# Transposes placed elsewhere in the first two chunks of a fused linear-attention and MLP kernel

## The chip, the cores and the metric

The kernel runs on one core of one Trainium2 chip. The metric is the device time of one execution in microseconds (us); the kernel before took 219.26 us, the median of 3 runs (218.94 to 219.39). Five engines work side by side, each through its own list of instructions in order: PE (matrix products and transposes), ACT (ScalarE: functions and copies), DVE (VectorE: elementwise work), POOL (GpSimd: elementwise work, and the issuing of loads) and SP (SyncE, which issues the first loads, the stores and some transposing transfers). They wait for each other by semaphores. PE writes only to PSUM, a small memory of eight banks, from which ACT and DVE read.

## The reference, cut to what matters

A linear attention with decay in blocks, and then a two-layer MLP with a periodic activation:

```python
batch, n_heads, seq, head_dim = (4, 8, 768, 64)      # q, k, v
n_tokens, d_model, d_ff = (3072, 512, 2048)          # the MLP
...
        intra = np.einsum('bhic,bhjc->bhij', qb, kb) * Dmask[None]
        intra = np.einsum('bhij,bhjd->bhid', intra, vb)
        inter = np.einsum('bhid,bhde->bhie', qb * lam_pow[None], kv_state)
        out[:, :, sl] = intra + inter
        ...
        kv_state = lam_block[None, :, None, None] * kv_state + np.einsum('bhsd,bhse->bhde', kb_dec, vb)
...
    h = x @ w_in
    s = np.sin(alpha * h)
    g = h + s * s / (alpha + 1e-09)
    return (g @ w_out).astype(np.float32)
```

## The kernel before

The sequence of 768 tokens is cut into six chunks of 128 tokens. One chunk of one of the four batches is called a unit, `u = 4 * chunk + batch`: units 0 to 3 are the first chunk, 4 to 7 the second. The program writes out the order of each engine by hand.

**A unit's attention.** `transposes(u)` (line 173) turns k and q of all eight heads by eight PE transposes, first four of k and then four of q, into one PSUM tile `QK_ps`, which ACT copies to `QKT` (line 183). `scores(u)` (line 196) makes eight products k times q into `F_ps` (PSUM tag `pf`), and DVE multiplies them with the decay mask to `STm` (line 209). `intra_mm(u)` (line 244) multiplies v with `STm` into `O_ps` (tag `po`), `inter_mm(u)` (line 254) adds q times the running state `kv`, and DVE's `copy_x(u)` (line 261) scales the sum into the unit's columns of `xt`, the input of the MLP. In the first chunk there is no state yet, and `first_out(u)` (line 345) does the products and the copy together.

**A chunk's MLP.** For a chunk `g` the 2048 hidden features are 16 slices ("sixteenths") of 128. `hidden(g, f)` (line 278) makes four products over the four batches' 512 tokens into a bank `hps`; ACT takes the sine (line 286) and, mostly, the square (line 289), and `finish(g, f)` (line 292) adds on DVE into `gall`. The banks for `hps` rotate, from the tenth sixteenth on over three tags h0, h1, h2 (line 275), so `hidden(f)` waits for `finish(f - 3)`. `project(g, n)` (line 305) multiplies `gall` with `w_out`; `hidden` of a chunk needs all of its `xt`.

**The start.** Until the first chunk's `xt` is complete there is no MLP work. k and q of unit 0 come through SP and are cast by DVE (lines 334 and 341); k, q and v of the others are loaded by POOL's queue, one after the other. Unit 0's k and q are transposed into a bank each and copied each for itself (lines 363 to 369); units 1 to 3 use `transposes`. `spin(n)` (line 356) issues n products of constants that nothing reads. ACT makes the table `Etab` (line 375) and, at line 379, loads the table of the sine ahead of its use. `a_ps` (line 387) is a small PE transpose of `alpha`, with the 16x16 identity `idf`; POOL makes `idf` (line 126) behind all the loads of the first chunk. DVE makes `alpha_sb` and `r_sb` from it (lines 392 and 394).

**The second chunk beside the first.** While `hidden(0, f)` runs, `slots(0)` (line 426) puts the second chunk's attention behind given sixteenths: `transposes` of unit 4 behind f = 7, unit 5 behind 8, unit 6 behind 12, and unit 7 behind 13, after `part_fo(None, 5)`, which is unit 5's `intra_mm` and `inter_mm`. `part_fo(6, None)`, unit 6's scores, stands behind 14. Behind f = 15 come `project(0, 0)`, unit 6's output with unit 7's scores, two more projections, unit 7's output and the fourth projection (lines 505 to 512), and then `hidden(1, 0)`. ACT follows the same order: the sine and the square of f, then the copy of the transposes that stand behind f. POOL's queue (`feed`, line 452) carries on with the decay of k, the loads and the state by itself. From the third chunk on, k and q are transposed by SP's transfers.

Of the kernel before, what the change touches and what calls it, by code (L numbers as in the profile page):

```python
# [9 lines left out]
ACTF = mybir.ActivationFunctionType  # L10
FP32 = mybir.dt.float32
# [4 lines left out]
def kernel(  # L16
# [11 lines left out]
    nc = tc.nc  # L28
    P = nc.NUM_PARTITIONS
# [15 lines left out]
    consts = ctx.enter_context(tc.tile_pool(name="consts", bufs=1))  # L45
# [25 lines left out]
    qn, kn, vn = {}, {}, {}  # L71
# [37 lines left out]
    iden = consts.tile([P, P], BF16, name="iden")  # L109
# [25 lines left out]
    for b in range(B):  # L135
# [3 lines left out]
    lnlam = consts.tile([P, H], FP32, name="lnlam")  # L139
# [3 lines left out]
                         func=ACTF.Exp, scale=pcol[:, 0:1])  # L143
# [17 lines left out]
    st = {u: {} for u in range(B * NT)}  # L161
# [11 lines left out]
    def transposes(u, tag="pqk"):  # L173
        t, b = divmod(u, B)
        QK_ps = psA.tile([P, 2, HP, T], BF16, name="QK_ps", tag=tag)
        for hp in range(HP):
            nc.tensor.transpose(out=QK_ps[:, 1, hp, :],
                                in_=kn[t][:, b, 2 * hp:2 * hp + 2, :], identity=iden[:])
        for hp in range(HP):
            nc.tensor.transpose(out=QK_ps[:, 0, hp, :],  # L180
                                in_=qn[t][:, b, 2 * hp:2 * hp + 2, :], identity=iden[:])
        QKT = qkp.tile([P, 2, HP, T], BF16, name="QKT")
        nc.scalar.copy(out=QKT[:], in_=QK_ps[:])  # L183
        st[u]["QT"], st[u]["KT"] = QKT[:, 0, :, :], QKT[:, 1, :, :]
# [11 lines left out]
    def scores(u, halves=1):  # L196
        QT, KT = st[u]["QT"], st[u]["KT"]
        F_ps = psA.tile([P, 2, HP, T], FP32, name="F_ps", tag="pf")
        for hp in range(HP):
            for hd in range(2):  # L200
                nc.tensor.matmul(out=F_ps[:, hd, hp, :],  # L201
                                 lhsT=KT[hd * D:(hd + 1) * D, hp, :],
                                 rhs=QT[hd * D:(hd + 1) * D, hp, :],
                                 start=True, stop=True)
        STm = work.tile([P, 2, HP, T], BF16, name="STm")
        n = HP // halves
        for s in range(halves):
            w = slice(s * n, (s + 1) * n)
            nc.vector.tensor_tensor(out=STm[:, :, w, :], in0=F_ps[:, :, w, :], in1=Cmask[:, :, w, :],  # L209
                                    op=ALU.mult)  # L210
        st[u]["STm"] = STm
# [63 lines left out]
    def h_tag(g, f):  # L275
        return f"h{(g * NFC + f) % 3}"
# [68 lines left out]
    def first_out(u, tag, hps_=range(4)):  # L345
        O_ps = psA.tile([P, HP, T], FP32, name="O_ps", tag=tag)
        for hp in hps_:
            for hd in range(2):
                nc.tensor.matmul(out=O_ps[hd * D:(hd + 1) * D, hp, :],
                                 lhsT=vn[0][:, u, 2 * hp + hd, :], rhs=st[u]["STm"][:, hd, hp, :],  # L350
                                 start=True, stop=True, skip_group_check=True)
        w = slice(hps_[0], hps_[-1] + 1)
        nc.vector.tensor_tensor(out=xt[0][:, w, u * T:(u + 1) * T], in0=O_ps[:, w, :],
                                in1=Etab[:, w, :], op=ALU.mult)

    def spin(n, cols=512):

        ps = psA.tile([P, GRP], FP32, name="hps", tag="h0")
        for _ in range(n):
            nc.tensor.matmul(out=ps[:, 0:cols], lhsT=fill[:, 0:P], rhs=fill[:, 0:cols], start=True, stop=True)  # L360

    spin(9)
    for nm, src, tag in (("KT", kn, "pqk"), ("QT", qn, "ops")):
        X_ps = psA.tile([P, HP, T], BF16, name="X_ps", tag=tag)
        for hp in range(HP):
            nc.tensor.transpose(out=X_ps[:, hp, :], in_=src[0][:, 0, 2 * hp:2 * hp + 2, :], identity=iden[:])
        XT = qkp.tile([P, HP, T], BF16, name=nm + "0")
        nc.scalar.copy(out=XT[:], in_=X_ps[:])
        st[0][nm] = XT[:]
        spin(3)  # L370
    scores(0)
    spin(1)
    transposes(1, "pqk")
    for hp in range(HP):
        nc.scalar.activation(out=Etab[:, hp, :], in_=pos_row[:], func=ACTF.Exp, scale=ln_hd[:, hp:hp + 1])
    spin(2)
    transposes(2, "ops")
    warm = consts.tile([P, 1], FP32, name="warm")
    nc.scalar.activation(out=warm[:], in_=lnlam[:, 0:1], func=ACTF.Sin)
    spin(1)  # L380
    scores(1)
    spin(1)
    first_out(0, "po")
    spin(1)
    scores(2)
    a_ps = psA.tile([P, NFC], FP32, name="a_ps", tag="h2")
    nc.tensor.transpose(out=a_ps[:], in_=alpha_fp[:], identity=idf[:])
    transposes(3, "pqk")
    spin(2)
    first_out(1, "h1")  # L390
    alpha_sb = consts.tile([P, NFC], FP32, name="alpha_sb")
    nc.vector.tensor_copy(out=alpha_sb[:], in_=a_ps[:])
    r_sb = consts.tile([P, NFC], FP32, name="r_sb")
    nc.vector.reciprocal(out=r_sb[:], in_=alpha_sb[:])
    spin(2)
    scores(3, 2)
    spin(1)
    first_out(2, "po")
    spin(2)
    first_out(3, "h1", range(0, 2))  # L400
    first_out(3, "ops", range(2, 4))
    spin(3)
# [23 lines left out]
    def slots(g):  # L426

        u = [B * (g + 1) + b for b in range(B)]
        T_, FO = transposes, part_fo
        if g == 0:  # L430
            return {3: [(part_k, (0, 1), "pf")], 6: [(part_k, (2, 3), "pf")],
                    7: [(T_, u[0])], 8: [(T_, u[1], "po")], 9: [(FO, u[0], None)],
                    11: [(FO, u[1], u[0]), (copy_x, u[0])], 12: [(T_, u[2])],
                    13: [(FO, None, u[1]), (T_, u[3], "ops"), (copy_x, u[1])], 14: [(FO, u[2], None)]}, {}
        if g == 1:
            return {4: [(part_k, (4, 5), h_tag(1, 5))], 6: [(part_k, (6, 7), h_tag(1, 7))],
                    8: [(FO, u[0], None)], 10: [(FO, u[1], u[0], h_tag(1, 11))],
                    12: [(FO, u[2], u[1], h_tag(1, 13))],
                    14: [(FO, u[3], u[2], h_tag(1, 15)), (copy_x, u[2])],
                    15: [(FO, None, u[3], h_tag(2, 0)), (copy_x, u[3])]}, {10: u[0], 12: u[1]}  # L440
        at = (3, 6, 9, 12, 14) if g == 2 else (1, 4, 7, 10, 13)
        tg = [h_tag(g, f + 1) if g < NT - 2 else None for f in at[1:]]
        return {at[0]: [(FO, u[0], None)], at[1]: [(FO, u[1], u[0], tg[0])], at[2]: [(FO, u[2], u[1], tg[1])],
                at[3]: [(FO, u[3], u[2], tg[2])], at[4]: [(FO, None, u[3], tg[3])]}, \
               {at[n + 1]: u[n] for n in range(4)}
# [30 lines left out]
    for g in range(NT + 1):  # L476
        if g < NT:
            gall[g] = gbp.tile([P, NFC, GRP], BF16, name="gall")
        at, xs = slots(g) if g + 1 < NT else ({}, {})
        fd = feed(g) if g + 1 < NT else {}  # L480
        if g + 1 < NT:
# [62 lines left out]
```

## Time and profile before

| what | value |
|---|---|
| median of 3 runs | 219.26 us (218.94 to 219.39) |
| the profiled execution's own time | 219.22 us |
| its span, first to last instruction | 217.5 us |
| PE busy | 208.3 us, 96% |
| ACT busy | 147.2 us, 68% |
| DVE busy | 126.6 us, 58% |
| POOL busy | 94.3 us, 43% |
| first product of `hidden(0, 0)` | 18.48 us |
| first product of `hidden(1, 0)` | 46.26 us |

All times within the execution are counted from the start of its span; what lies outside the span is 219.22 - 217.5 = 1.72 us. A line of the timeline gives a group's start, its length, engine, line of the kernel, operation, output and inputs, and the number of instructions; in brackets stands how long the engine was idle before it, and what ended that. [...]

### The profile page before, as it was taken

Reading aid. Unit: us, or ns where it says so; the run is one execution under the profiler, and the core shown is the slowest. Engines: PE = TensorE matmul, PEld = TensorE weight load, DVE = VectorE, ACT = ScalarE, POOL = GpSimd, SP = SyncE. Lnnn points to the kernel's source line nnn. Section 1 sums busy time; section 2 is a strip of 40 time slices with the busy share of each in tenths; the row PEclk is TensorE's granted clock in tenths of the full one; section 3 lists DMA queues with packets and bytes.
Section 4 is the critical chain, followed back from the end, with each engine's and each line's share of the span. In section 5 each row is a group of like instructions: output and inputs, shape, how many; then the busy total and the mean of one; then the engine's idle time right before and its main releaser. Section 6 shows DMA issues by size and latency. Waiting matters only on the chain.

```text
span 217.5 us, 3864 instructions
## 1 busy us (share of the span) xinstructions
PE 208.3 (96%) x1504; PEld 99.6 (46%) x1504; DVE 126.6 (58%) x183; ACT 147.2 (68%) x234; POOL 94.3 (43%) x131
## 2 busy tenths in 40 slices
PE   7799986999999999999999999999999999999994
PEld 2354443544444544445454444444444444444453
DVE  4576977834656875567656777545767544444300
ACT  5573998728766648766667675777676779787521
POOL 7999999963899569052474611100000000000000
PEclk9999999999999999999999999999999999999999
DMA  5999999999999999929689990490110101111022
GB/s 102 150 158 198 176 167 184 208 175 154 197 176 136 177 148 139 189 46 135 143 101 124 166 119 29 116 128 21 75 50 3 48 0 48 51 50 48 0 101 96
DMA packets 99747, 24.65 MB, mean 113 GB/s; under 512 B 91904, under 2 KB 96784, under 8 KB 99728
## 3 DMA queue, kind: packets, MB, share of 16 engines
q0 software_dynamic: 76976, 13.37, 79.0%
q1 hardware_dynamic: 22752, 11.03, 23.6%
q8 instruction: 12, 0.20, 0.4%
q14 instruction: 7, 0.06, 0.1%
HBM read 27.28 MB, written 6.29 MB: 154 GB/s over the span
## 4 chain that ended last, share of the span: by engine, by line
PE 78%; POOL 10%; DMA 5%; ACT 2%; issue 2%; DVE 1%; POOLq 0%; ACTq 0%
PE ops L311 36%; PE hps L283 32%; DMA qn<-in_q_dram 5%; PE O_ps L257 3%; PE F_ps L201 2%; POOL vn L87 2%; PE O_ps L249 2%; POOL kdec L170 2%; POOL qn L87 2%; POOL w_in L93 2%; PE KVA_ps L220 2%; PE hps L325 2%; POOL kn L87 2%; ACT s_sb L286 1%; ACT s L289 1%
## 5 line engine op out<-in xcount | busy, mean ns | idle before, releaser
L296 DVE SCALAR_TENSOR_TENSOR gall<-s,r_sb,hps 128x512 bf16<-128x512 bf16 x96 | 71.2, 745 | 67.0 <-ACT s L289 66.7
L286 ACT ACTIVATE s_sb<-hps,alpha_sb 128x512 bf16<-128x512 f32 x96 | 65.8, 687 | 49.7 <-PE hps L283 49.7
L283 PE MATMUL hps<-xt,w_in 128*128 128x512 bf16 x384 | 97.6, 379 | 0.1
L311 PE MATMUL ops<-w_out,gall 128*128 128x512 bf16 x368 | 93.0, 379 | 0.0
L289 ACT ACTIVATE s<-s_sb 128x512 bf16<-128x512 bf16 x92 | 58.0, 630 | 3.0
L283 PEld LDWEIGHTS <-w_in 128*128 128x128 bf16 x384 | 36.9, 98 | 44.3 <-DVE kvs L229 0.9
L311 PEld LDWEIGHTS <-gall 128*128 128x128 bf16 x368 | 34.8, 98 | 38.3
L235 POOL CAST kv<-kvs 64x256 bf16<-64x256 f32 x40 | 16.0, 401 | 41.8 <-PE O_ps L257 36.8
L209 DVE TENSOR_TENSOR STm<-F_ps,Cmask 128x1024 bf16<-128x1024 f32 (+1 forms) x25 | 29.4, 1178 | 3.8 <-PE F_ps L201 3.1
L170 POOL TENSOR_TENSOR kdec<-kn,Rtok 128x512 bf16<-128x512 bf16 x20 | 20.9, 1065 | 2.8 <-DMA kn<-in_k_dram 2.5
L316 ACT COPY o_sb<-ops 128x512 f32<-128x512 f32 x23 | 13.2, 572 | 6.4 <-PE ops L311 6.4
L263 DVE TENSOR_TENSOR xt<-O_ps,Etab 128x512 bf16<-128x512 f32 x20 | 13.7, 684 | 1.7 <-PE O_ps L257 1.6
L87 POOL DMA_DIRECT2D vn<-in_v_dram x12 | 14.2, 1195 | 0.0
L87 POOL DMA_DIRECT2D kn<-in_k_dram x11 | 13.5, 1227 | 0.3 <-issue 0.3
L87 POOL DMA_DIRECT2D qn<-in_q_dram x11 | 13.3, 1206 | 0.0
L360 PE MATMUL hps<-fill 128*128 128x512 bf16 x31 | 10.8, 455 | 1.5 <-DVE fill L112 1.5
L241 POOL TENSOR_TENSOR kvd<-kvs,L 128x256 f32<-128x256 f32 x16 | 9.8, 615 | 1.0
L249 PE MATMUL O_ps<-STm,vn 128*64 128x128 bf16 x160 | 8.0, 222 | 1.1 <-DVE STm L209 0.6
L183 ACT COPY QKT<-QK_ps 128x1024 bf16<-128x1024 bf16 x7 | 7.0, 1002 | 2.0 <-PE QK_ps L180 1.9
L249 PEld LDWEIGHTS <-vn 128*64 128x64 bf16 x160 | 5.3, 110 | 4.5 <-issue 3.5
L220 PEld LDWEIGHTS <-kdec 128*64 128x64 bf16 x160 | 3.8, 111 | 6.8 <-issue 6.4
L201 PE MATMUL F_ps<-QT,KT 64*128 64x128 bf16 x136 | 6.8, 219 | 0.0
(61 smaller groups left out, 84.5 us busy)
## 6 DMA issues: line engine op xcount, KB each, us to landing
out_dram<-o_sb SPq DMA_DIRECT2D x23, 256.0 KB, 2.7
w_out<-in_moe_w_out_dram POOLq DMA_DIRECT2D x4, 512.0 KB, 14.0
w_in<-in_moe_w_in_dram POOLq DMA_DIRECT2D x3, 512.0 KB, 9.5
kn<-in_k_dram POOLq DMA_DIRECT2D x6, 256.0 KB, 10.9
qn<-in_q_dram POOLq DMA_DIRECT2D x6, 256.0 KB, 11.3
vn<-in_v_dram POOLq DMA_DIRECT2D x6, 256.0 KB, 11.3
kn<-in_k_dram POOLq DMA_DIRECT2D x2, 512.0 KB, 7.5
qn<-in_q_dram POOLq DMA_DIRECT2D x2, 512.0 KB, 8.5
```

Of the source, the lines that this page charges most:

```text
L87: nc.gpsimd.dma_start(out=dst[t][:, b0:b1, :, :].rearrange("p b h e -> p (b h) e"), in_=src[b0:b1, :, t * T:(t + 1) * T, :].rearrange("b h ...
L170: nc.gpsimd.tensor_tensor(out=kdec[:], in0=kn[t][:, b, :, :], in1=head_bc(Rtok), op=ALU.mult)
L209: nc.vector.tensor_tensor(out=STm[:, :, w, :], in0=F_ps[:, :, w, :], in1=Cmask[:, :, w, :], op=ALU.mult)
L235: nc.gpsimd.tensor_copy(out=kv[b][s, :, hd, :], in_=kvs[u][s, :, :])
L249: nc.tensor.matmul(out=O_ps[hd * D:(hd + 1) * D, hp, :], lhsT=vn[t][:, b, 2 * hp + hd, :], rhs=st[u]["STm"][:, hd, hp, :], start=(hp == 0) ...
L263: nc.vector.tensor_tensor(out=xt[t][:, :, b * T:(b + 1) * T], in0=st[u]["O_ps"][:], in1=Etab[:], op=ALU.mult)
L283: nc.tensor.matmul(out=hps[:], lhsT=w_in_of[f][:, c, :], rhs=xt[g][:, c, :], start=(c == 0), stop=(c == NDC - 1))
L286: nc.scalar.activation(out=s_sb[:], in_=hps[:], func=ACTF.Sin, scale=alpha_sb[:, f:f + 1])
L289: nc.scalar.activation(out=s2[:], in_=s_sb[:], func=ACTF.Square)
L296: nc.vector.scalar_tensor_tensor(out=gall[g][:, f, :], in0=s2[:], scalar=r_sb[:, f:f + 1], in1=hps[:], op0=ALU.mult, op1=ALU.add)
L311: nc.tensor.matmul(out=ops[:], lhsT=gall[g][:, f, m * P:(m + 1) * P], rhs=w_out_sb[part][:, f % 4, :], start=(f == 0), stop=(f == NFC - 1))
L316: nc.scalar.copy(out=o_sb[:], in_=ops[:])
```

## The change

Two things are written differently; no arithmetic changes. In the first chunk, `half_T` transposes k or q of one unit into a bank of its own and ACT copies it by itself. It now serves units 0, 1 and 3; unit 2 still uses `transposes`. The order of the start is new with it: unit 1's k is turned before unit 0's scores, the transpose `a_ps` and its two DVE operations stand ahead of unit 1's scores instead of behind unit 2's, the sine's table load stands behind unit 2's copy and ahead of unit 3's two, and unit 2's scores stand behind unit 1's output. There are 29 spin products instead of 31. In the second chunk, `transposes` of unit 6 stands no longer behind the sixteenth f = 12 but behind f = 13, after unit 5's output and just ahead of unit 7's. The lists of POOL and SP are as before.

```diff
-    spin(9)
-    for nm, src, tag in (("KT", kn, "pqk"), ("QT", qn, "ops")):
+    def half_T(u, nm, tag):
+
+        src = {"KT": kn, "QT": qn}[nm]
         X_ps = psA.tile([P, HP, T], BF16, name="X_ps", tag=tag)
         for hp in range(HP):
-            nc.tensor.transpose(out=X_ps[:, hp, :], in_=src[0][:, 0, 2 * hp:2 * hp + 2, :], identity=iden[:])
+            nc.tensor.transpose(out=X_ps[:, hp, :], in_=src[0][:, u, 2 * hp:2 * hp + 2, :], identity=iden[:])
         XT = qkp.tile([P, HP, T], BF16, name=nm + "0")
         nc.scalar.copy(out=XT[:], in_=X_ps[:])
-        st[0][nm] = XT[:]
-        spin(3)
+        st[u][nm] = XT[:]
+
+    spin(9)
+    half_T(0, "KT", "pqk")
+    spin(3)
+    half_T(0, "QT", "ops")
+    spin(1)
+    half_T(1, "KT", "pqk")
+    spin(1)
     scores(0)
-    spin(1)
-    transposes(1, "pqk")
+    half_T(1, "QT", "ops")
     for hp in range(HP):
         nc.scalar.activation(out=Etab[:, hp, :], in_=pos_row[:], func=ACTF.Exp, scale=ln_hd[:, hp:hp + 1])
-    spin(2)
-    transposes(2, "ops")
-    warm = consts.tile([P, 1], FP32, name="warm")
-    nc.scalar.activation(out=warm[:], in_=lnlam[:, 0:1], func=ACTF.Sin)
-    spin(1)
-    scores(1)
-    spin(1)
-    first_out(0, "po")
-    spin(1)
-    scores(2)
     a_ps = psA.tile([P, NFC], FP32, name="a_ps", tag="h2")
     nc.tensor.transpose(out=a_ps[:], in_=alpha_fp[:], identity=idf[:])
-    transposes(3, "pqk")
-    spin(2)
-    first_out(1, "h1")
     alpha_sb = consts.tile([P, NFC], FP32, name="alpha_sb")
     nc.vector.tensor_copy(out=alpha_sb[:], in_=a_ps[:])
     r_sb = consts.tile([P, NFC], FP32, name="r_sb")
     nc.vector.reciprocal(out=r_sb[:], in_=alpha_sb[:])
     spin(2)
-    scores(3, 2)
+    scores(1)
+    spin(1)
+    transposes(2, "pqk")
+    warm = consts.tile([P, 1], FP32, name="warm")
+    nc.scalar.activation(out=warm[:], in_=lnlam[:, 0:1], func=ACTF.Sin)
+    spin(1)
+    first_out(0, "po")
+    spin(2)
+    first_out(1, "h1")
+    scores(2)
+    half_T(3, "KT", "ops")
+    spin(1)
+    half_T(3, "QT", "pqk")
     spin(1)
     first_out(2, "po")
-    spin(2)
+    scores(3, 2)
+    spin(4)
     first_out(3, "h1", range(0, 2))
     first_out(3, "ops", range(2, 4))
     spin(3)
...
-                    11: [(FO, u[1], u[0]), (copy_x, u[0])], 12: [(T_, u[2])],
-                    13: [(FO, None, u[1]), (T_, u[3], "ops"), (copy_x, u[1])], 14: [(FO, u[2], None)]}, {}
+                    11: [(FO, u[1], u[0]), (copy_x, u[0])],
+                    13: [(FO, None, u[1]), (copy_x, u[1]), (T_, u[2]), (T_, u[3], "ops")],
+                    14: [(FO, u[2], None)]}, {}
```

## The prediction, written before the changed kernel was run

> **What bounds the kernel now.** I read the page's chain first: 78% of the span is PE. The waits and stage table next: from 45.5 us on PE waits for nothing (168.75 of 172.00 us busy). So whatever moves the start of `hidden(1, 0)`, at 46.26, moves the end by as much, and all that counts lies before it. Then I read each engine's timeline up to there. The second chunk's part:
>
> ```profile
> 33.03 1.02 PE L283 MATMUL hps<-xt,w_in 128*128 128x512 bf16 x4
> 34.51 0.40 PE L177 MATMUL QK_ps<-iden,kn 128*128 128x128 bf16 x4 [0.46 <-DMA kn<-in_k_dram]
> 36.08 0.40 PE L180 MATMUL QK_ps<-iden,qn 128*128 128x128 bf16 x4 [1.17 <-DMA qn<-in_q_dram]
> ...
> 37.27 0.41 PE L249 MATMUL O_ps<-STm,vn 128*64 128x128 bf16 x8
> 37.62 0.40 PE L257 MATMUL O_ps<-QKT,kv 128*128 128x128 bf16 x4
> 37.85 0.39 PE L177 MATMUL QK_ps<-iden,kn 128*128 128x128 bf16 x4
> ```
>
> PE stands 0.46 + 1.17 = 1.63 us in unit 6's transposes until its k and q land. But ACT, which does sine and square of every sixteenth, loses less:
>
> ```profile
> 35.28 0.63 ACT L289 ACTIVATE s<-s_sb 128x512 bf16<-128x512 bf16 x1
> 36.51 1.01 ACT L183 COPY QKT<-QK_ps 128x1024 bf16<-128x1024 bf16 x1 [0.61 <-PE QK_ps L180]
> 37.42 0.69 ACT L286 ACTIVATE s_sb<-hps,alpha_sb 128x512 bf16<-128x512 f32 x1
> ```
>
> It was still busy until 35.9, is idle 0.61 us, and is then never idle until its last square ends at 42.17. On that hang DVE's last sum, unit 7's mask at 42.87, unit 6's `xt` at 44.01, PE at 44.74, and `hidden(1, 0)`. ACT's idle time, not PE's, is what this stage can win.
>
> The start:
>
> ```profile
> 8.39 0.40 PE L201 MATMUL F_ps<-QT,KT 64*128 64x128 bf16 x8
> 8.72 0.39 PE L360 MATMUL hps<-fill 128*128 128x512 bf16 x1
> 8.95 0.39 PE L177 MATMUL QK_ps<-iden,kn 128*128 128x128 bf16 x4
> ...
> 13.51 0.23 PE L387 MATMUL a_ps<-idf,alpha_fp 16*128 16x16 f32 x1
> ```
>
> ```profile
> 9.59 1.80 POOL L87 DMA_DIRECT2D vn<-in_v_dram  x2
> 11.32 0.10 POOL masks.py:197 MEMSET idf<- 16x16 f32 x1
> 11.50 0.19 POOL masks.py:199 TENSOR_SCALAR_AFFINE_SELECT idf<-idf 16x16 f32<-16x16 f32 x1
> 11.72 3.00 POOL L93 DMA_DIRECT2D w_in<-in_moe_w_in_dram  x4
> ```
>
> `idf`, which `a_ps` reads, is there only at 11.69, since POOL issues the first chunk's loads ahead of it without a pause. Before, `a_ps` came at 13.51 and did not notice.
>
> **The start, step by step.** POOL's list is unchanged, so its times stay. Spacings are start to start, from PE's timeline.
>
> 1. Unit 0 as before to its q at 7.32. One spin instead of three (0.22), unit 1's k at 7.77, a spin, and unit 0's scores still at 8.39, since they wait for the copy of q (7.75 + 0.59). Unit 1's q at 8.72 (it landed at 2.48 + 5.7 = 8.2). Its copy ends by 9.15 + 0.59 = 9.74; `Etab` takes ACT to 10.9. All of this is hidden.
> 2. `a_ps` is next on PE, at 8.95, and must wait for `idf`: 11.69 + 0.05 (what other releases of PE take: 8.34 to 8.39) = 11.74. PE stands 2.8 us, with everything behind it. Bounds: nothing, if `idf` were there, and 2.8; I take 2.8, as the same instructions of POOL set it.
> 3. `a_ps` 0.16 (13.51 to 13.68), two spins 0.54 (15.01 to 15.54): unit 1's scores at 12.44, against 11.46 before. Mask 0.44 later (8.39 to 8.83): 12.88 to 14.10. DVE's two on `alpha` (0.17 and 0.25) fall before it, between 12.0 and 12.5, where DVE idles.
> 4. Scores 0.33, spin 0.23: unit 2's k at 13.00, q at 13.22; ACT's copy 0.43 later, 13.65 to 14.65. Then the table load (1.28) and its use (0.20), which stood in a gap at 12.69 before and now stand ahead of unit 3's copies: to 16.17. Unit 3's two copies end at about 17.2.
> 5. PE: spin, unit 0's output at 13.77, two spins, unit 1's at 14.64, unit 2's scores at 14.99. DVE: unit 0's `xt` 14.23 to 14.91 (0.46 after its products, 0.68 long), unit 1's 15.10 to 15.79, unit 2's mask 15.71 to 16.93. Unit 2's output waits for that: 16.98.
> 6. Unit 3's scores at 17.33: unit 2's products take 0.35, and the copy at 17.2 is just in time. Unit 2's `xt` 17.44 to 18.12, unit 3's two masks 18.04 to 19.26 (1.22). The four spins (17.66 to 18.6) hide behind them.
> 7. From the end of these masks to `hidden(0, 0)` before: 18.48 - 17.31 = 1.17. Now 19.26 + 1.17 = 20.43. The start is 1.95 us longer.
>
> The two spins fewer, and copies in halves (four of 0.59 for two of 1.01: 0.3 us more on ACT), cost nothing: ACT has gaps until 13.65 and the last pair is counted in step 4.
>
> **The second chunk.** Without any delay from the start: `hidden(0, 13)` is not held by the transposes, but by its bank: `finish(10)` ends at 34.21, so it runs at 34.26. Unit 5's output waits for the bank of unit 4's (35.26 + 0.68 = 35.94): 35.99 instead of 37.27. Unit 6's transposes follow 0.58 later at 36.57, q at 36.79; q landed at 24.34 + 11.7 = 36.0, so there is no wait. ACT takes f = 13 at 35.82 and 36.54, is free at 37.08 and gets unit 6's copy at 36.79 + 0.43 = 37.22: 0.14 idle. Unit 7's copy at 38.11, sine of f = 14 at 39.00 instead of 39.58. All behind moves by 0.58: the last mask, `xt`, `hidden(1, 0)`. `project(0, 0)` would wait for `w_out` (28.44 + 11.3 = 39.7), which PE has time for. No DMA is issued by the moved step, and SP's and POOL's queues are not passed. Bounds: nothing, and PE's whole 1.63; I take 0.58, as ACT's timeline carries the end.
>
> After the delay of the start, everything in this stage that ACT sets comes 1.95 later, and the sum is 1.95 - 0.58 = 1.37. The loads land when they did; unit 6's transposes at their old place would then no longer wait, and ACT's 0.61 idle us would be gone without the move (1.95 - 0.61 = 1.34). So the second part by itself is worth 0.6, and behind the first one nothing.
>
> **Sum:** 219.22 + 1.37 = 220.6 us against the profiled execution, whose time is 0.04 under the median, less than any term here.
>
> **The clock.** A PE that stands may be slowed. In this trace the first nine spins take 0.43 us each (4.02 for nine), later ones 0.22. In 33.00 to 36.40 PE was busy 1.77 of 3.40 us and kept the full clock; in 213.90 to 217.20 it was busy 0.35 of 3.30 us and the granted clock was 0.50 at 217.30. In the new start, 3.4 us around the wait would hold some 0.8 us of work: between the two. If the clock halves at about 12.0 for 3.4 us, steps 3 and 4 stretch: two spins and scores 12.87, unit 2's transposes to 14.76, its copy 14.95 (1.3 later), unit 3's at 18.55, masks to 20.84, `hidden(0, 0)` at 22.0: 1.6 us more. Bounds 0 and, for two such stretches, 3.2; I take 0, because the wait is shorter than the stretch. [...]
>
> **The rivals.**
> - *The clock drops* in the wait (above): 222.2. For it the row at 217.30, against it that of 33.00 to 36.40. It may differ from execution to execution.
> - *`idf` is in time*, and the kernel is faster. If POOL's work on it is over sooner than its spans say (they are rough), `a_ps` costs 0.16, unit 1's scores follow unit 0's mask at 10.1, and by steps 3 to 7 unit 3's q (landed 8.72 + 5.1 = 13.8) sets the end as before: `hidden(0, 0)` at about 18.4, and the sum is 219.22 - 0.58 - 0.1 = 218.5. The wait moves the end one for one, so it decides below 11.69 - 1.37 = 10.3 us. Against it: two v loads hold POOL until 11.39.
> - *The second chunk wins PE's whole 1.63* and pays for the start: 219.22 + 1.95 - 1.63 = 219.5. ACT's unbroken timeline speaks against it.
>
> **Chances.** My sum 0.62 (alone 220.1 to 221.0: each step's spacing can be 0.1 off), clock 0.28, `idf` in time 0.05, offset 0.05. The range leaves out the faster rival and most of the offset at the bottom, and a second slow stretch at the top: 219.7 to 222.4. A change under 0.2% (0.44 us) cannot be told from none here: faster 0.06, same 0.05, slower 0.89.
>
> **What the new profile should show.** PE idle about 2.8 us ahead of `a_ps`, released by POOL at 11.7; unit 3's copies behind the table load, ending near 17.2; `hidden(0, 0)` near 20.4; no DMA wait in unit 6's transposes; `hidden(1, 0)` near 47.6; PE unbroken after it. I am wrong if `a_ps` does not wait, if spins after it are 0.43 us apart, or if the late start is given back behind 20.4.

## The result and the profile after

The changed kernel takes 222.16 us, the median of 7 executions (220.65 to 223.06), against 219.26 us before (now the median of 7 executions, 218.94 to 219.59); the ratio is 1.0126 (95% interval 1.0100 to 1.0151). It is slower, as forecast, but by 2.9 us where 1.3 was the forecast. The seven executions lie in three groups, and the mean clock granted to PE, which each execution's records give, sorts them:

| executions | time in us | mean granted clock |
|---|---|---|
| 2 | 220.65, 220.86 | 0.999 |
| 3 | 222.01, 222.16, 222.31 | 0.991 to 0.992 |
| 2 | 223.05, 223.06 | 0.985 |

The execution whose profile follows took 222.01 us and belongs to the second group. From the page of the changed kernel, two of the rows in 40 slices of 5.5 us, PE's busy tenths and its granted clock; the third slice has 6 tenths:

```profile
PE   6588998889999999999999999999999999999994
PEclk9969999999999999999999999999999999999999
```

PE's timeline of the start, changed kernel (a group can start before the listed length of the one ahead is over, as the transposes at 8.70 do behind the 0.40 us from 8.36):

```profile
8.36 0.40 PE L201 MATMUL F_ps<-QT,KT 64*128 64x128 bf16 x8
8.70 0.40 PE L367 MATMUL X_ps<-iden,qn 128*128 128x128 bf16 x4
11.70 0.28 PE L384 MATMUL a_ps<-idf,alpha_fp 16*128 16x16 f32 x1 [2.61 <-POOL idf masks.py:199]
11.92 1.03 PE L360 MATMUL hps<-fill 128*128 128x512 bf16 x2
12.88 0.61 PE L201 MATMUL F_ps<-QT,KT 64*128 64x128 bf16 x8
13.43 0.61 PE L360 MATMUL hps<-fill 128*128 128x512 bf16 x1
13.82 0.63 PE L177 MATMUL QK_ps<-iden,kn 128*128 128x128 bf16 x4
...
18.30 0.41 PE L349 MATMUL O_ps<-STm,vn 128*64 128x128 bf16 x8 [0.60 <-DVE STm L209]
18.65 0.40 PE L201 MATMUL F_ps<-QT,KT 64*128 64x128 bf16 x8
...
21.80 3.61 PE L283 MATMUL hps<-xt,w_in 128*128 128x512 bf16 x16
...
49.06 1.02 PE L283 MATMUL hps<-xt,w_in 128*128 128x512 bf16 x3
```

The last two are `hidden(0, 0)` and `hidden(1, 0)`. In the kernel before they are:

```profile
18.48 3.61 PE L283 MATMUL hps<-xt,w_in 128*128 128x512 bf16 x16
...
46.26 1.02 PE L283 MATMUL hps<-xt,w_in 128*128 128x512 bf16 x4
```

The wait is where the prediction put it: `a_ps` stands until POOL has made `idf`. (The 2.61 us in brackets count from the listed end of the group before, at 9.10; the prediction's 2.8 count from 8.95, where `a_ps` would have started.) Behind it the lengths are different. Unit 1's scores are listed with 0.61 us where unit 0's have 0.40, the transposes with 0.63 instead of 0.39. A spin takes 0.39 us, from 13.43 to 13.82, instead of 0.22; spins that far apart are a sign that the prediction had named for being wrong. The table of stages says why. Its columns are the stretch, its length, the busy time of PE, PE's weight loads, DVE, ACT and POOL with the number of instructions, then PE's granted clock, the DMA share and GB/s:

```profile
8.04:11.45 3.41, 1.03 (x15) 0.54 (x12) 1.55 (x2) 2.52 (x7) 3.35 (x5) 1.00 2.46 146
11.46:14.87 3.41, 3.17 (x21) 1.68 (x21) 1.65 (x3) 0.00 (x0) 3.37 (x6) 0.50 2.12 135
14.87:18.28 3.41, 2.68 (x37) 1.56 (x37) 2.51 (x3) 3.33 (x5) 3.41 (x4) 1.00 1.24 161
```

PE was busy 1.03 of the 3.41 us before 11.46, and then ran at half clock for 3.41 us. In those it did 21 products; experiment 2, which keeps its clock, does 40 in the same stretch (shown below). ACT had nothing to do in them, and its unit 2 copy and table load came late, ahead of unit 3's copies:

```profile
14.92 1.01 ACT L183 COPY QKT<-QK_ps 128x1024 bf16<-128x1024 bf16 x1 [4.03 <-PE QK_ps L180]
15.95 1.28 ACT L394 ACT_TABLE_LOAD   x1
17.25 0.20 ACT L394 ACTIVATE warm<-lnlam 128x1 f32<-128x1 f32 x1
17.36 0.57 ACT L369 COPY KT<-X_ps 128x512 bf16<-128x512 bf16 x1
17.82 0.59 ACT L369 COPY QT<-X_ps 128x512 bf16<-128x512 bf16 x1
```

`hidden(0, 0)` starts at 21.80 us, 3.32 later than before. The second chunk gives 0.52 of it back (21.80 to 49.06 is 27.26 us; before, 18.48 to 46.26 was 27.78), so `hidden(1, 0)` comes 2.80 later, and the execution takes 222.01 instead of 219.22 us, 2.79 more. Nothing is won or lost behind it.

Unit 6's part of the second chunk, PE's timeline of the changed kernel:

```profile
39.32 0.41 PE L249 MATMUL O_ps<-STm,vn 128*64 128x128 bf16 x8 [0.71 <-DVE xt L263]
39.67 0.40 PE L257 MATMUL O_ps<-QKT,kv 128*128 128x128 bf16 x4
39.90 0.39 PE L177 MATMUL QK_ps<-iden,kn 128*128 128x128 bf16 x4
40.12 0.39 PE L180 MATMUL QK_ps<-iden,qn 128*128 128x128 bf16 x4
```

No transpose waits for a load any more; PE waits for the bank of unit 4's output instead, as worked out, and it costs nothing: ACT, which sets the pace, stands only 0.08 us ahead of unit 6's copy (its square ends at 40.47, the copy starts at 40.55).

### The profile page after: what moved, and what is told of

It reads as the page before. It is cut to its first block, busy times and chain, and to the rows that moved or that the text cites. A ratio compares the mean times of both kernels' runs of the same rounds, so it can differ in the third digit from the quotient of the medians.

```text
span 220.3 us, 3836 instructions
## 1 busy us (share of the span) xinstructions
PE 206.7 (94%) x1475; PEld 100.4 (46%) x1502; DVE 126.4 (57%) x183; ACT 147.2 (67%) x236; POOL 93.9 (43%) x131
## 4 chain that ended last, share of the span: by engine, by line
PE 81%; DVE 6%; POOL 4%; ACT 4%; issue 3%; ACTq 0%; POOLq 0%
PE ops L311 35%; PE hps L283 32%; PE O_ps L257 3%; PE F_ps L201 3%; PE O_ps L249 2%; DVE STm L209 2%; DVE gall L296 2%; ACT s_sb L286 2%; PE KVA_ps L220 2%; PE hps L325 2%; POOL vn L87 2%; PE hps L360 1%; POOL qn L87 1%; ACT QKT L183 1%; ACT s L289 1%
## 5 line engine op out<-in xcount | busy, mean ns | idle before, releaser
L311 PE MATMUL ops<-w_out,gall 128*128 128x512 bf16 x354 | 91.0, 379 | 0.8
L360 PE MATMUL hps<-fill 128*128 128x512 bf16 x27 | 10.3, 477 | 1.6 <-DVE fill L112 1.5
L201 PE MATMUL F_ps<-QT,KT 64*128 64x128 bf16 x152 | 7.8, 223 | 0.0
L183 ACT COPY QKT<-QK_ps 128x1024 bf16<-128x1024 bf16 x5 | 4.9, 1006 | 4.1 <-PE QK_ps L180 4.0
```

The source lines that it names most:

```text
L201: nc.tensor.matmul(out=F_ps[:, hd, hp, :], lhsT=KT[hd * D:(hd + 1) * D, hp, :], rhs=QT[hd * D:(hd + 1) * D, hp, :], start=True, stop=True)
L311: nc.tensor.matmul(out=ops[:], lhsT=gall[g][:, f, m * P:(m + 1) * P], rhs=w_out_sb[part][:, f % 4, :], start=(f == 0), stop=(f == NFC - 1))
```

## The experiments

The theory had by now two halves: the wait for `idf` delays the start, and the half clock that follows it in most executions (5 of 7 by the mean clock) is the rest. Rivals were that the new order loses by itself, that the clock falls for another reason, and other prices for the second part. Every kernel below computes the whole output. Each ratio is to the kernel before on the same chip: the first four kernels shared one chip (median before 218.92 us, 27 executions), the next four another (218.95, 27), the last three a third (219.09, 29). The changed kernel was not measured again beside them. The ratios are not the quotients of the medians, and differ from them by up to 0.3%.

**1. Alpha late.** The changed kernel, with the six lines of `a_ps`, `alpha_sb` and `r_sb` put behind unit 2's scores:

```diff
-    a_ps = psA.tile([P, NFC], FP32, name="a_ps", tag="h2")
...
     scores(2)
+    a_ps = psA.tile([P, NFC], FP32, name="a_ps", tag="h2")
+    nc.tensor.transpose(out=a_ps[:], in_=alpha_fp[:], identity=idf[:])
...
     half_T(3, "KT", "ops")
```

> The changed kernel, with the transpose of alpha and its two DVE operations put behind unit 2's scores again, and nothing else. Theory (PE's wait for idf, and the half clock that follows it, are the whole loss): no wait for idf, no half clock before the end, hidden(0, 0) near 18.3 us, unit 6's transposes without a wait, 218.4 us (218.1 to 218.8), faster than the kernel before by some 0.8 us. Rival (the new order and the copies in halves lose by themselves, above all the table load ahead of unit 3's copies): hidden(0, 0) later than 19 us and 220 us or more.

Measured: 219.22 us (218.50 to 219.97, 12 executions), ratio 1.0001 (0.9978 to 1.0024); the clock is 0.999 or 1.000 in all. `hidden(0, 0)` comes at 18.22 and `hidden(1, 0)` at 45.52, in a profiled execution of 218.50 us. PE's timeline:

```profile
8.95 0.60 PE L360 MATMUL hps<-fill 128*128 128x512 bf16 x2
10.19 0.40 PE L201 MATMUL F_ps<-QT,KT 64*128 64x128 bf16 x8 [0.65 <-DVE STm L209]
...
13.06 0.23 PE L395 MATMUL a_ps<-idf,alpha_fp 16*128 16x16 f32 x1
...
18.22 3.61 PE L283 MATMUL hps<-xt,w_in 128*128 128x512 bf16 x16
```

The whole loss goes with the wait for `idf`, though table load and halves of copies stay where the change put them: the rival is out. But the 0.8 us that I expected to win is there only in the profiled execution (218.50 us, against the 219.22 of the first profile), not in the median. Experiments 3 and 5 look for it.

**2. Spins in the wait.** The changed kernel, with PE kept at work until `idf` comes:

```diff
+    spin(12)
     a_ps = psA.tile([P, NFC], FP32, name="a_ps", tag="h2")
```

> The changed kernel, with 12 spin products (12 x 0.22 = 2.6 us) in front of the transpose of alpha: PE works through the time in which it waits for idf, and idf comes no sooner. Theory (standing idle halves the clock): no execution loses clock before its end, hidden(0, 0) at 20.4 us, and all executions lie together at 220.6 to 220.9 us. Rival (the clock falls for another reason, such as fewer spins later in the start): times spread from 220.7 to 223 as in the changed kernel, with a granted clock of 0.985 to 0.992.

Measured: 220.72 us (220.64 to 220.96, 10 executions), ratio 1.0075 (1.0052 to 1.0098). No execution lost clock; all lie within 0.32 us, where the changed kernel spread over 2.41. PE's timeline and the stage table's rows:

```profile
8.94 2.54 PE L360 MATMUL hps<-fill 128*128 128x512 bf16 x11
11.72 0.23 PE L385 MATMUL a_ps<-idf,alpha_fp 16*128 16x16 f32 x1 [0.24 <-POOL idf masks.py:199]
11.88 0.61 PE L360 MATMUL hps<-fill 128*128 128x512 bf16 x2
12.42 0.40 PE L201 MATMUL F_ps<-QT,KT 64*128 64x128 bf16 x8
...
20.45 3.61 PE L283 MATMUL hps<-xt,w_in 128*128 128x512 bf16 x16
```

```profile
8.04:11.45 3.41, 3.39 (x26) 1.63 (x24) 1.56 (x2) 2.53 (x7) 3.36 (x5) 1.00 2.59 151
11.46:14.87 3.41, 3.17 (x40) 1.69 (x39) 2.27 (x4) 1.23 (x2) 3.36 (x6) 1.00 2.54 154
```

`idf` comes no sooner and the spins compute nothing that is read, and yet the median is 1.4 us below the changed kernel's, where that kernel's own two executions that kept their clock lie (220.65 and 220.86). With PE's idle time filled, the half clock is gone in all 10 executions (0.998 to 1.000): the standing idle is what brought it here. (One of the 12 spin records is missing from the trace.)

**3. The second part alone.** The kernel before with the new `slots(0)`:

```diff
-                    11: [(FO, u[1], u[0]), (copy_x, u[0])], 12: [(T_, u[2])],
-                    13: [(FO, None, u[1]), (T_, u[3], "ops"), (copy_x, u[1])], 14: [(FO, u[2], None)]}, {}
+                    11: [(FO, u[1], u[0]), (copy_x, u[0])],
+                    13: [(FO, None, u[1]), (copy_x, u[1]), (T_, u[2]), (T_, u[3], "ops")],
+                    14: [(FO, u[2], None)]}, {}
```

> The kernel before, with unit 6's transposes behind the sixteenth 13 only. Theory (ACT sets the end of this stage and was idle 0.61 us): hidden(1, 0) 0.58 us earlier, at 45.7, and 218.65 us. Rival 1 (PE's 1.63 us of waiting come off): 217.6 us. Rival 2 (the wait is given back elsewhere): 219.2 us.

Measured: 219.08 us (218.52 to 219.32, 12 executions), ratio 0.9996 (0.9975 to 1.0017). The profiled execution took 218.52 us, with `hidden(1, 0)` at 45.55 and ACT idle 0.08 us ahead of unit 6's copy, as the theory has it; the median does not show it: a gain of 0.58 us lies just outside the interval, whose lower end is 0.55 us under the kernel before. Rival 1 is out; rival 2 is not, by this run.

**4. The first part alone.** The changed kernel with the old `slots(0)`, the same diff the other way round.

> The changed kernel, with unit 6's transposes behind the sixteenth 12 as before. Theory (the late start alone takes away the wait for unit 6's k and q, so that the second part is worth nothing behind it): like the changed kernel within 0.2 us at the same clock, 220.6 us where the clock is kept and 222.2 where it is halved once. Rival (the second part is worth 0.58 there too): 221.2 where the clock is kept, 222.8 where it is halved once.

Measured: 221.90 us (220.81 to 222.16, 6 executions). One kept the clock, 220.81 us, against 220.65 and 220.86 for the changed kernel; five had 0.992, at 221.52 to 222.16, against 222.01 to 222.31. So behind the late start the second part is worth nothing, within some 0.3 us; of the rival's 221.2 and 222.8 nothing is seen. The execution that kept the clock was the profiled one, and it tells more. With the old order PE waits 0.18 us for unit 6's q there, and `hidden(1, 0)` comes 27.05 us behind `hidden(0, 0)` (20.67 to 47.72), no later than the 27.26 of the changed kernel. In the wait for `idf` PE stood nearly as long as in the changed kernel, but the clock's stretches lay otherwise:

```profile
11.94 0.23 PE L384 MATMUL a_ps<-idf,alpha_fp 16*128 16x16 f32 x1 [2.49 <-POOL idf masks.py:199]
```

```profile
7.56:10.97 3.41, 1.78 (x22) 1.14 (x22) 2.39 (x3) 2.55 (x7) 3.41 (x5) 1.00 2.37 151
10.97:14.38 3.41, 2.44 (x30) 1.41 (x31) 1.65 (x3) 0.81 (x2) 3.30 (x7) 1.00 2.17 136
```

In this execution's trace the clock rises to full at 7.55 (11 products fill the whole 3.30 us from 4.10 to 7.40); in the changed kernel's it rises at 4.63, falls at 11.46 and rises again at 14.87, so that the changes are 2 and 1 times 3.41 us apart, and in the first profile they are 62 times 3.41 us apart (5.67 to 217.30). Counted on like that, which is my estimate, a boundary at 10.97 fell into the middle of the wait here, 9.45 to 11.94, and neither stretch was less than half busy (52% and 72%). In the changed kernel the fall at 11.46 cut off only the last 0.24 us of the wait, 9.10 to 11.70.

**5. The kernel before once more,** for its own profile beside experiment 3. No edit.

> The kernel before, unchanged, for its own profile beside that of the second part alone (218.52 us in its profiled execution, but a median of 219.08 against 218.92). Theory (what the second part wins is ACT's idle time while unit 6's q lands, so that it is worth only as much as that q is late): where q lands 0.5 us earlier than in the first profile, ACT's idle time ahead of unit 6's copy is 0.1 us instead of 0.61, hidden(1, 0) comes at 45.7 and the execution takes 218.6 us. Rival (the gain is lost later): ACT idle 0.6 us and hidden(1, 0) at 46.2 in an execution of 219.2 us, and executions of 218.5 are not explained by this stage.

Measured: 219.00 us (218.36 to 221.28, 12 executions), on its chip equal to the kernel before (1.0002), as it must be. In its profiled execution, of 218.81 us, PE and ACT show:

```profile
35.58 0.40 PE L180 MATMUL QK_ps<-iden,qn 128*128 128x128 bf16 x4 [1.27 <-DMA qn<-in_q_dram]
```

```profile
35.32 0.63 ACT L289 ACTIVATE s<-s_sb 128x512 bf16<-128x512 bf16 x1
36.02 1.01 ACT L183 COPY QKT<-QK_ps 128x1024 bf16<-128x1024 bf16 x1
```

PE waits 1.27 us for unit 6's q here too, but q came at 35.58 instead of 36.08, and ACT was busy until 35.95: next to nothing is idle (0.07 us), and `hidden(1, 0)` comes at 45.76. So the kernel before takes 218.8 us by itself where q lands early, and the second part's worth is how late q lands past ACT: 0.61 us in the first profile less the 0.08 that experiment 3 still has, some 0.5; nothing in this one. The time from `hidden(0, 0)` to `hidden(1, 0)` agrees: 27.78 us in the first profile, 27.25 in experiment 3, and 27.45 here, where ACT began unit 4's copy 0.2 us later behind the square before it than in experiment 3 (27.09 to 27.82, against 27.08 to 27.62). That, and the theory's expectation, agree; how often q is late was not counted, and that the medians of experiments 1 and 3 show no gain is explained by this only as far as two profiles go.

**6 and 7. Two and five spins in the wait,** instead of twelve. The diff of 6; in 7 it is `spin(5)`.

```diff
+    spin(2)
     a_ps = psA.tile([P, NFC], FP32, name="a_ps", tag="h2")
```

> The changed kernel with 2 spin products in front of the transpose of alpha: PE stands 2.17 us instead of 2.6, so that the emptiest 3.41 us hold 36% of work instead of some 25%. If the clock needs nearly empty stretches, all executions lie at 220.6 to 220.9; if it is halved wherever less than about half of a stretch is busy, some 6 in 10 executions are near 222.1, the others near 220.7.

> The same with 5 spin products: PE stands 1.5 us, and the emptiest 3.41 us hold 55% of work, about as much as the busy 52% of 33.00 to 36.40 us in the kernel before, which kept the clock. Both theories: 220.6 to 220.9 in all executions. If some are near 222, the clock falls even at half of the work.

Measured: with two spins 222.15 us (220.65 to 222.40, 5 executions): four at clock 0.991 to 0.992 and 222.14 to 222.40, one at 1.000 and 220.65. With five 220.65 us (220.62 to 220.82, 10 executions), ratio 1.0066 (1.0045 to 1.0087), clock 0.998 to 1.000 in all. The stage table of two spins, its profiled execution having been of the slower kind, and then of five, over the emptiest 3.41 us I could find (in the 3.41 us from 8.65 and from 9.00 it is 1.88 us, 55% too):

```profile
9.55:12.96 3.41, 0.99 (x11) 0.47 (x11) 0.43 (x2) 0.85 (x3) 3.30 (x7) 1.00 2.25 143
12.97:16.37 3.40, 3.04 (x25) 1.58 (x22) 1.91 (x2) 1.85 (x2) 3.40 (x5) 0.50 1.61 143
```

```profile
8.30:11.71 3.41, 1.86 (x19) 0.93 (x18) 1.28 (x2) 2.26 (x7) 3.30 (x7) 1.00 2.45 149
```

The stop, 1.53 us in the profiled execution, cost none of the ten its clock. With two spins the clock was lost in four of five executions. The stop was to be 2.2 us; in the profiled execution it was 2.93, since PE came to it earlier and `idf` was ready later, at 11.97, and in the others it is not known. But a stretch 29% busy lost the clock here too, and that kills the assumption that only a nearly empty stretch counts.

**8. A faster version.** Alpha late, one spin instead of three before `hidden(0, 0)`, and the loads of units 4 and 5 ahead of `w_in`'s fourth piece:

```diff
-    for i in range(4):
+    for i in range(3):
         load_w_in(i)
...
     load(1, 1, 0, 2)
+    load_w_in(3)
     load_w_in(4)
...
     first_out(3, "ops", range(2, 4))
-    spin(3)
+    spin(1)
```

> The changed kernel with alpha's transpose behind unit 2's scores, one spin instead of three ahead of hidden(0, 0), and POOL's loads of the second chunk's first k and q ahead of the fourth piece of w_in. The two spins stand behind the last masks on the way to hidden(0, 0): 0.4 us less, if unit 4's q no longer holds ACT. Theory: hidden(0, 0) near 17.8, 218.2 us in executions without other delays, 0.2 to 0.4 us below the version with alpha late. Rival (w_in's fourth piece lands too late, near 27, and ACT waits for hidden(0, 8)): no gain, 219.0 or more.

Measured: 218.53 us (218.18 to 219.48, 12 executions), ratio 0.9969 (0.9948 to 0.9990): 0.4 us below the kernel before in the medians. Its profiled execution was its slowest, 219.48 us; PE waited there 1.28 us for a piece of `w_in` ahead of `hidden(0, 0)`, which came at 18.68.

**9, 10 and 11. Its two edits apart, and both again.**

> The version with alpha late and one spin instead of three ahead of hidden(0, 0), with POOL's loads as before. Theory (both edits of the faster version are needed: unit 4's q, which lands near 27.1, holds ACT as soon as the start is earlier): hidden(0, 0) near 17.8, ACT idle 0.3 to 0.4 us ahead of unit 4's copy, 218.9 us or within 0.15 of the version with alpha late. Rival (the two spins alone are the gain): as fast as the version with both edits.

> The version with alpha late and the loads of unit 4 and 5's k and q ahead of w_in's fourth piece, with three spins. Theory: hidden(0, 0) stays near 18.2 behind the spins and ACT had no idle time at unit 4's copy there, so nothing is won: 218.9 us or within 0.15 of the version with alpha late. Rival (the loads alone are the gain): as fast as the version with both edits.

> The version with both edits once more, beside each by itself and on their chip: 0.3 us below the kernel before, and 0.3 below each edit alone if both are needed.

Measured: one spin alone 219.10 us, ratio 0.9999 (0.9976 to 1.0022); the loads alone 218.95 us, 0.9982 (0.9958 to 1.0006); both 218.69 us, 0.9983 (0.9964 to 1.0002). With one spin alone, ACT stands at unit 4's copy, more than was expected, as q landed later, at 27.7:

```profile
28.16 1.01 ACT L183 COPY QKT<-QK_ps 128x1024 bf16<-128x1024 bf16 x1 [0.78 <-PE QK_ps L180]
```

With both edits `hidden(0, 0)` comes at 17.62, and the next limit shows on PE: the piece of `w_in` that the loads have passed.

```profile
27.90 1.04 PE L284 MATMUL hps<-xt,w_in 128*128 128x512 bf16 x4 [1.38 <-DMA w_in<-in_moe_w_in_dram]
```

In this execution `hidden(1, 0)` came at 46.19, so nothing of the earlier start was left by then (46.26 in the first profile).

So the spins alone win nothing that these runs can tell. The loads alone and both together cannot be told apart from each other, nor, on this chip, surely from the kernel before; the two measurements of both edits put the gain at 0.4 us in the medians (0.7 and 0.4 by the ratios), with an interval that once leaves out no change and once just includes it.

## Why the prediction was right and where it was wrong

Step by step, start times in us (the sixth line is an end), beside experiment 2, where PE keeps its clock and `idf` comes when it does, and the changed kernel's profile:

| step | predicted | spins in the wait | changed kernel, half clock |
|---|---|---|---|
| `a_ps` | 11.74 | 11.72 | 11.70 |
| unit 1's scores | 12.44 | 12.42 | 12.88 |
| unit 2's k on PE | 13.00 | 12.97 | 13.82 |
| ACT's copy of unit 2 | 13.65 | 13.62 | 14.92 |
| unit 2's output | 16.98 | 16.95 | 18.30 |
| unit 3's last copy ends | 17.2 | 17.11 | 18.41 |
| unit 3's scores | 17.33 | 17.29 | 18.65 |
| `hidden(0, 0)` | 20.43 | 20.45 | 21.80 |
| `hidden(1, 0)` | 47.6 | 47.70 | 49.06 |
| the execution | 220.6 | 220.65 | 222.01 |

- **The wait for `idf`, and each spacing behind it** (steps 1 to 7): right, within 0.1 us. Read from POOL's unchanged list and start-to-start spacings of the kernel before, they needed no run.
- **The second chunk's 0.58:** 0.52 here, in the kernel's own execution. Right too that ACT and not PE holds it, and that behind the late start it is worth nothing (experiment 4). What I did not see is that the 0.61 us of ACT's idle time belonged to that execution: the kernel before has executions in which it is 0.07 (experiment 5), so the term is not 0.58 but something between 0 and that. Experiments 2 and 7, which kept their clock, lie 1.8 and 1.7 us above the kernel before in the medians (1.6 and 1.4 by the ratios), where the sum without the clock is 1.37. The difference is of a size that this term can explain; no run isolates it.
- **The clock: this is the step that failed.** Its price was near: 1.6 us was written for one slow stretch of 3.4 us, a length that no run had shown by then (the changed kernel's trace has 3.41), and `hidden(0, 0)` at 22.0; the profile has 21.80, 1.35 us behind experiment 2's, and the median of the changed kernel is 1.4 above experiment 2's, so 1.4 us measured. What was wrong is "I take 0, because the wait is shorter than the stretch", and with it the chance of 0.28. No run shows that it is enough for a wait to be shorter: the one of 2.61 us lost the clock in the changed kernel's profile, the one of 2.49 us kept it in experiment 4's. Counting by mean clock, the changed kernel lost it in 5 of 7 executions, its first part alone in 5 of 6, against none of 10 with twelve spins. So the likeliest time was that of the rival, 222.2, and the measured median is 222.16. That the two agree to 0.04 is partly luck, since the rival's price was 0.2 too large.
- **Why that step failed.** I weighed two rows, one stretch 52% busy that kept the clock and one some 10% busy that lost it, and let the new one, 24% by my count, go with the first for a reason that neither showed. In these runs a stretch that lost the clock need not have been idle. Lost: 1.03 of 3.41 us (30%), 0.99 of 3.41 (29%), and at the ends of two executions 36% and 42%, below. Kept: 1.78 of 3.41 (52%) in experiment 4, and the first of the two rows (52%), which runs from 8 to 9 times 3.413 us behind the clock's rise at 5.67. So the busiest of these that lost it was at 42%, the emptiest that kept it at 52%. A stretch 42% busy (1.42 of 3.40 us) has 1.98 us in which PE stands; my estimate from that is that a stop was enough here if some 2 us of it fell into one stretch that was otherwise busy: 2.36 us did in the changed kernel's profile, which lost the clock, and 1.5 in experiment 4's, which kept it.
- **The two executions at 223.05 us and clock 0.985** fit two slow stretches: 3.41 us at half clock take 1.71 us off 221.3, which is 0.992, and twice that is 0.985. They cost 0.9 us more than the second group, where the prediction's upper bound gave the second stretch 1.6. No trace of one was taken.

The two rows that I weighed, from the stage table of the kernel before, with the clock behind the second:

```profile
33.00:36.40 3.40, 1.77 (x17) 0.87 (x14) 2.94 (x4) 2.84 (x5) 3.30 (x4) 1.00 2.04 177
213.90:217.20 3.30, 0.35 (x4) 0.07 (x1) 0.00 (x0) 0.37 (x1) 0.00 (x0) 1.00 0.23 81
217.30:217.50 0.20, 0.00 (x0) 0.00 (x0) 0.00 (x0) 0.00 (x0) 0.00 (x0) 0.50 0.00 0
```

The other ends, which I had not thought to read: PE's last products lie in a stretch that is part busy, and the clock afterwards shows what it was worth. Stage table of the loads alone (experiment 10), of the kernel before again (5) and of five spins (7), each up to the fall of the clock and behind it (in the last no fall shows up to the span's end, and I chose the place of the stretch):

```profile
212.82:216.22 3.40, 1.42 (x13) 1.02 (x11) 0.00 (x0) 0.49 (x2) 0.00 (x0) 1.00 0.27 90
216.24:217.50 1.26, 0.00 (x0) 0.00 (x0) 0.00 (x0) 0.00 (x0) 0.00 (x0) 0.50 0.00 0
```

```profile
212.52:215.92 3.40, 1.22 (x12) 0.85 (x9) 0.00 (x0) 0.37 (x1) 0.00 (x0) 1.00 0.24 81
215.94:217.00 1.06, 0.00 (x0) 0.00 (x0) 0.00 (x0) 0.00 (x0) 0.00 (x0) 0.50 0.00 0
```

```profile
213.63:217.03 3.40, 2.02 (x19) 1.56 (x16) 0.00 (x0) 0.74 (x2) 0.00 (x0) 1.00 0.33 120
217.04:218.90 1.86, 0.00 (x0) 0.00 (x0) 0.00 (x0) 0.00 (x0) 0.00 (x0) 1.00 0.17 61
```

With 42% and 36% busy the clock was at 0.50 behind the stretch, with 59% at 1.00.

## What to carry to other kernels

Before an instruction is moved forward, look up when its least conspicuous operand is made: here a 16x16 identity behind ten loads in POOL's list held PE for 2.6 us. Price a stop of PE twice, by its own length and by the clock behind it: a stretch of 3.41 us that was 30% busy cost another 1.4 us here, and five unread products (1.1 us of work) in the stop removed that price. And take an engine's idle time as the worth of a change only after a second execution shows it too, if a transfer ends it.

## What the runs showed of the hardware that was not expected

The half clock lasted one stretch of 3.41 us in both traces that show it in the start: from 11.46 to 14.87 in the changed kernel, and from 12.97 to 16.37 with two spins, where the mean clock of 0.992 leaves room for no more. The first two profiles put multiples of 3.41 us between changes (62 of full clock before, from 5.67 to 217.30; 2, 1 and 60 in the changed kernel, from 4.63 over 11.46 and 14.87 to 219.67). The first rise lies differently in each of three executions (5.67, 4.63, and 7.55 in experiment 4), and one kernel has times 1.4 us apart (the changed kernel, 220.65 and 220.86 against 222.01 to 222.31); of the first part alone one execution kept the clock, with 2.5 us of standing idle, and five did not; that these five differ by where their boundaries lay is argued from the profiled one, since none of the five was traced. The kernel before has a few such executions as well, 5 of the 95 whose clock is on record, at 220.8 to 221.4 us with a mean clock of 0.990 to 0.992; none of them was traced, and why they happen is open.
